# Five staging tiles instead of two for made weights, and their making spread over 49 or 50 steps of a block

## The chip, the cores and the metric

The kernel runs on one core of a Trainium2 chip. The metric is the device time of one execution in microseconds (us), median of several runs. A profile is one further execution, with its own time.

## The reference, cut to what matters

Attention with random features (4 batches, 8 heads, 576 positions, 64 per head) gives 2304 tokens of 512 numbers. Two layers follow, each with a hidden width of 2048:

```python
def reference(**kwargs):
    attn_out = _attn_ref(**attn_kwargs)
    x = np.ascontiguousarray(attn_out.transpose(0, 2, 1, 3)).reshape(B * S, H * D)
    x = _moe_ref(x=x, **moe_kwargs)       # h = x @ w_in; g = max(h,0) + alpha*min(h,0); g @ w_out
    return _moe2_ref(x=x, **moe2_kwargs)  # h = x @ w_in; r = max(h,0); (r*r) @ w_out
```

The weights w_in and w_out of both layers arrive as 64-bit numbers. The kernel turns them into 32-bit numbers by itself, and each number into a rounded part and a rest (hi and lo), so that three products on TensorE take the place of one exact product.

## The kernel before

**Blocks, turns, steps.** The 2304 tokens are three blocks of 768. A layer's hidden width is eight pairs of 256. The first layer runs three blocks (k = 0, 1, 2) of eight turns, one pair in each turn. In blocks 1 and 2 a turn has seven steps: seven products of 384 columns (a 2 by 2 scheme with seven instead of eight products, with operands such as A11, S1, T1), 42 matmuls in all, and between them the matmuls of the second product (`mm2`) of the pair before, 10 parts by the table `FILL`. So a block is 56 steps, numbered `turn * 7 + m`. Steps 1, 4 and 6 of a turn each have one VectorE (DVE) addition c = h + s, which reads a PSUM tile that a later product needs; ScalarE (ACT) copies s out of PSUM in steps 0, 2 and 4. Then come ReLU (ACT), slope r (DVE), high part gh (ACT) and rest gl (DVE), and `mm2` reads gh and gl.

**Order.** Every engine runs its instructions in the order in which the program writes them (`manual_schedule`). One DMA queue, SyncE's (SP), issues nearly all transfers, also in program order; raw weights are loaded by GpSimd's (POOL) queue into the part of x that is free in this block.

**Making weights.** Beside the matmuls the kernel makes the weights. `UNITS` lists the units of work; 9 to 16 are made in block 1, and 17 to 24 in block 2 (`ENDS`), all for the second layer. A unit loads two raw tiles of 512 KB (128 x 1024 x 4 bytes), scales and merges them to 32 bits (ACT, DVE, POOL), forms four sums, and so has eight matrices of 128 x 256. Seven of them are split into hi and lo (`cast` on ACT, `rest` on DVE) into a staging tile, and the staging tile is written to memory by SP (`keep`, `keep3`). A unit has ten positions (`SHORT`); `put(at, ...)` says what is done at which position. The staging tiles are `ma` (three matrices) and `ms` (four): `ma` is written at positions 5 to 8 and saved at 8; `ms` is written at 10 to 13 and saved at 13. The next unit's first cast into `ma` is at position 15, that into `ms` at 20; each must wait until the save has landed.

**Pace.** In blocks 1 and 2 the call of `upto` decides how many positions are done by each step:

```python
            elif layer == 0 and k and turn * 7 + m > (0, 5, 3)[k]:
                upto(end_of(ENDS[k - 1]) + (end_of(ENDS[k]) - end_of(ENDS[k - 1])) * (turn * 7 + m - (0, 5, 3)[k]) // (0, 44, 46)[k],
                     ENDS[k], k)
```

so the 80 positions of a block's eight units lie in steps 5 to 49 (block 1) and 3 to 49 (block 2).

**Reading.** In each turn whose next pair isn't held, SP reads that pair's made weights back: two halves of 896 KB and two of 512 KB. Turn 8 (`turn` 7) of block 1 reads nothing, since block 2 walks its pairs in the opposite direction.

**Operands of the next block.** The table `NEXT[1]` adds to steps 45 to 58 four differences (DVE), seven casts xh (ACT) and seven rests xl (DVE) of 768 columns, for the products of the block that follows. In the first turn of that block the result y is copied to x by ACT and DVE (line 904).

Of the kernel before, what the change touches and what calls it, by code (L numbers as in the profile page):

```python
# [10 lines left out]
F32R = mybir.dt.float32r  # L11
# [7 lines left out]
P = 128  # L19
# [16 lines left out]
QW = 2 * P  # L36
# [11 lines left out]
ENDS = (9, 17, 25)  # L48
# [6 lines left out]
def tile_performer_moe(ctx, tc, qt, kt, qn, kn, vn, omt, w1i, w1o, al, w2i, w2o, out):  # L55
# [38 lines left out]
    class Raw:  # L94
# [37 lines left out]
        def merge(self):  # L132
            nc.vector.scalar_tensor_tensor(
                out=self.high, in0=self.high, scalar=-0x80000000, in1=self.t, op0=ALU.bitwise_and, op1=ALU.bitwise_or)
            nc.gpsimd.tensor_tensor(out=self.out.bitcast(I32), in0=self.high, in1=self.low, op=ALU.add)  # L135

    def sums(names, outer=False):
        w = tiles["wf1"]
        a21, a22, a11, a12, s1, s2, s3, s4 = (w[:, n] for n in range(8))
        todo = {1: (s1, a21, a22, ALU.add), 2: (s2, s1, a11, ALU.subtract),  # L140
                3: (s3, a11, a21, ALU.subtract), 4: (s4, a12, s2, ALU.subtract)}
        if outer:

            b21, b22, b11, b12, t1, t2, t3, t4 = (w[:, n] for n in range(8))
            todo = {1: (t1, b12, b11, ALU.subtract), 2: (t2, b22, t1, ALU.subtract),
                    3: (t3, b22, b12, ALU.subtract), 4: (t4, b21, t2, ALU.subtract)}
        for n in names:
            o, a, b, op = todo[n]
            nc.vector.tensor_tensor(out=o, in0=a, in1=b, op=op)  # L149
# [6 lines left out]
    def made():  # L156
# [19 lines left out]
        def merge(raw):  # L176
            raw.merge()
            raws.remove(raw)
            fetch()
# [5 lines left out]
        def first(key, u, a0, a1):  # L185

            layer, p = key
            if layer == 0:
                return ring[p % 2][0][:, u, a0:a1]
            return tiles["ma"][:, u, a0 - A22:a1 - A22] if a1 <= S1 else tiles["ms"][:, u, a0 - S1:a1 - S1]  # L190

        def second(key, u, i):
            return ring[key[1] % 2][1][:, u, i]
# [7 lines left out]
        def keep(key, which, at, tile, queue=nc.sync):  # L201
            queue.dma_start(out=kept[key][which][:, :, at].bitcast(F32), in_=tile.bitcast(F32))

            if at in (0, slice(0, 7), slice(3, 7)):
                done.add((key, which))

        f1, f2 = tiles["wf1"], tiles["wf2"]

        def third(a0, a1):
            n, a = ("ma", 0) if a1 <= 3 else ("ms", 4)  # L210
            t = tiles[n].rearrange("p u n q -> p (u n q)").rearrange("p (n u q) -> p n u q", u=2, q=QW)
            return t[:, a0 - a:a1 - a]

        def cast3(a0, a1):
            high(third(a0, a1)[:, :, 0], f1[:, a0:a1])
# [5 lines left out]
        def keep3(p, a0, a1):  # L221
            n0 = a0 if a1 <= 3 else a0 - 1
            nc.sync.dma_start(out=outer[:, n0:n0 + a1 - a0, p].bitcast(F32), in_=third(a0, a1).bitcast(F32))
            done.add(((1, p), 1, n0))

        def cast1(key, a0, a1):
            high(first(key, 0, a0, a1), f1[:, a0:a1])

        def rest1(key, a0, a1):
            low(first(key, 1, a0, a1), f1[:, a0:a1], first(key, 0, a0, a1))  # L230
# [56 lines left out]
        def plan_unit(n, base):  # L287

            n1, n2 = UNITS[n]
            a, b = ((0, 0), (0, 1)) if n1 else ((1, 1), (1, 0))  # L290

            def put(at, *what):
                schedule[base + at] += what

            if n1:
                cast, rest, keeps = (lambda *r: cast1(n1, *r)), (lambda *r: rest1(n1, *r)), [
                    lambda: keep(n1, 0, slice(0, 3), tiles["ma"]), lambda: keep(n1, 0, slice(3, 7), tiles["ms"])]
                first_, second_ = (A11, S1), (A22, A11)
            else:
                cast, rest, keeps = cast3, rest3, [lambda: keep3(n2[1], 0, 3), lambda: keep3(n2[1], 4, 8)]  # L300
                first_, second_ = (0, 2), (2, 3)
            put(-1 if n not in ENDS else 0, lambda: used[n, *a].scale_high())
            put(0, lambda: used[n, *a].scale_low(), lambda: used[n, *a].shift())
            put(2, lambda: merge(used[n, *a]))
            put(3, lambda: used[n, *b].scale_high())
            put(4, lambda: used[n, *b].scale_low(), lambda: used[n, *b].shift())
            put(5, lambda: merge(used[n, *b]), lambda: cast(*first_))
            put(6, lambda: rest(*first_))
            put(7, lambda: cast(*second_), lambda: sums((1, 2), not n1))
            put(8, lambda: rest(*second_), keeps[0])  # L310
            put(9, lambda: sums((3, 4), not n1))
            put(10, lambda: cast(S1, S3))
            put(11, lambda: cast(S3, 8), lambda: rest(S1, S3))
            put(13, lambda: rest(S3, 8), keeps[1])

        for n in range(NPAIR + 1, len(UNITS)):
            plan_unit(n, (n - NPAIR - 1) * SHORT)
# [18 lines left out]
    def end_of(n):  # L336
        return min(n, NPAIR + 1) * STAGES + max(n - NPAIR - 1, 0) * SHORT + (4 if n == len(UNITS) else 0)
# [6 lines left out]
    def upto(where, most, blk):  # L344

        while position[0] < min(where, end_of(most)):
            onward(most, blk)
# [44 lines left out]
    def cast(k, n, of=operand):  # L392
        nc.scalar.copy(out=tiles["xh", n], in_=of(k, n))

    def rest(k, n, of=operand):
        nc.vector.tensor_tensor(out=tiles["xl", n], in0=of(k, n), in1=tiles["xh", n].bitcast(F32), op=ALU.subtract)  # L396
# [519 lines left out]
        for c in ("xh", "xl"):  # L916
            tiles[c, n] = xp.tile([P, 2, HB], F32R, name=f"{c}{n}")
    mr = making_room.enter_context(tc.tile_pool(name="mr", bufs=1, side="right", reuse_waits="tile"))
    for n, a in (("ma", 3), ("ms", 4)):
        tiles[n] = mr.tile([P, 2, a, QW], F32R, name=n)  # L920
    ring_end = ctx.enter_context(ExitStack())
    wp = ring_end.enter_context(tc.tile_pool(name="w2p", bufs=1, reuse_waits="tile"))
    ring[1].append(wp.tile([P, 2, 2, DM], F32R, name="w2_1"))
# [14 lines left out]
    for n, (layer, k, turn, p) in enumerate(plan):  # L938
        lead = plan[n + 1] if n + 1 < len(plan) else None
        held[p % 2] = layer, p  # L940
        reading = lead and lead[:2] != (0, 0) and held[lead[3] % 2] != (lead[0], lead[3])
        if layer:
            making_room.close()
            values(0)
        fill = enumerate(mm2(*before)) if before else iter(())
        full = []
        first = (layer, k) == (0, 0)
        steps = stepping.pop() if stepping else plain(p) if first else pair(layer, p)
        for m, got in enumerate(steps, DRAINED if n == 0 else 0):
            if reading and m in (0, 2):  # L950
                read(lead[0], lead[3], 0, m // 2)
            if layer and m == 0:
                for part in GROUPS:
                    read_pair(0, 1, part)
            if first and turn:

                upto((p + 1) * STAGES + STAGES * (m + 1) // 8 + 1, ENDS[0], 0)
            elif layer == 0 and k and turn * 7 + m > (0, 5, 3)[k]:
                upto(end_of(ENDS[k - 1]) + (end_of(ENDS[k]) - end_of(ENDS[k - 1])) * (turn * 7 + m - (0, 5, 3)[k]) // (0, 44, 46)[k],
                     ENDS[k], k)  # L960
            elif layer == 0 and k and m == (0, 5, 3)[k]:
                ask(ENDS[k], k)
            elif (layer, k, turn) == (0, 1, 0) and m < 2:

                onward(ENDS[0], 0)
            for blk, at in ((n // NPAIR, turn * (8 if first else 7) + m), (n // NPAIR - 1, NPAIR * 7 + turn * 7 + m)):

                table = NEXT[0 if blk == 0 else 1]
                at -= (NPAIR - 1) * (8 if blk == 0 and first else 7)
                if blk == 0 and not first:  # L970
                    at += 1
                if 0 <= blk < BLOCKS:
                    for what, operand_ in table.get(at, ()):
                        what((blk + 1) % BLOCKS, operand_)
            for rows in full:
                evacuate(ended, y, rows)
            full = []
            for _ in range(FILL[0 if first else 1][m]):
                part, _ = next(fill, (None, None))
                if turn == 0 and part is not None and part in COMPLETE:  # L980
                    full.append(COMPLETE[part])
        for part, _ in fill:
            if turn == 0 and part in COMPLETE:
                full.append(COMPLETE[part])
        for rows in full:
            evacuate(ended, y, rows)
        if turn == 0 and not layer:
            y = [py.tile([P, 512], F32, name=f"y{c}") for c in range(NB // P)]
        if reading and lead[0] == 0:
            read(lead[0], lead[3], 1, 1)  # L990
            read(lead[0], lead[3], 1, 0)
        before = turn, p, *got, y
        ended = k
# [281 lines left out]
```

## Time and profile before

| | |
|---|---|
| time, median of 3 runs | 905.99 us (902.18 to 906.78) |
| time of the profiled execution | 901.07 us, span 899.0 us |
| mean granted clock | 0.997 |
| TensorE (PE) busy | 881.9 us, 98% |
| VectorE (DVE), ScalarE (ACT), GpSimd (POOL) busy | 673.4, 522.6, 166.2 us |
| DMA | 228.81 MB, mean 255 GB/s |

PE's busy time counts a matmul from its start to a modelled end. What the kernel could win on PE is in its gaps, and a gap is read by what ended it, and by what that in turn waited for.

### The profile page before, as it was taken

Reading aid. Unit: us, or ns where it says so; the run is one execution under the profiler, and the core shown is the slowest. Engines: PE = TensorE matmul, PEld = TensorE weight load, DVE = VectorE, ACT = ScalarE, POOL = GpSimd, SP = SyncE. Lnnn points to the kernel's source line nnn. Section 1 sums busy time; section 2 is a strip of 40 time slices with the busy share of each in tenths; the row PEclk is TensorE's granted clock in tenths of the full one; section 3 lists DMA queues with packets and bytes.
Section 4 is the critical chain, followed back from the end, with each engine's and each line's share of the span. In section 5 each row is a group of like instructions: output and inputs, shape, how many; then the busy total and the mean of one; then the engine's idle time right before and its main releaser. Section 6 shows DMA issues by size and latency. Waiting matters only on the chain.

```text
span 899.0 us, 18473 instructions
## 1 busy us (share of the span) xinstructions
PE 881.9 (98%) x7328; PEld 834.8 (93%) x7328; DVE 673.4 (75%) x1077; ACT 522.6 (58%) x1109; POOL 166.2 (18%) x192
## 2 busy tenths in 40 slices
PE   9999999999999999999999999999999999999998
PEld 7998889999998888898898999999999999999998
DVE  5868987998986887877788974668855688657674
ACT  6889886777676666667676753334523245333432
POOL 6642322444412322202232100000000000000000
PEclk9999999999999999999999999999999999999999
DMA  7644316898836999927999975767697686876763
GB/s 272 196 139 144 120 30 219 293 303 284 291 141 227 348 399 375 337 92 291 393 348 366 369 266 168 249 249 264 235 309 250 205 322 251 268 259 228 297 249 135
DMA packets 82293, 228.81 MB, mean 255 GB/s; under 512 B 6176, under 2 KB 16800, under 8 KB 77216
## 3 DMA queue, kind: packets, MB, share of 16 engines
q1 hardware_dynamic: 72640, 192.21, 59.7%
q0 software_dynamic: 9216, 33.56, 11.2%
q10 hardware_dynamic: 352, 1.87, 0.6%
q8 instruction: 58, 0.95, 0.4%
q14 instruction: 27, 0.22, 0.1%
HBM read 170.47 MB, written 57.15 MB: 253 GB/s over the span
## 4 chain that ended last, share of the span: by engine, by line
PE 52%; DMA 2%; DVE 2%; ACT 1%; issue 0%; ACTq 0%; DVEq 0%
PE h L717 15%; PE sumb L717 10%; PE suma L1075 9%; PE sumc L1075 8%; PE y L886 7%; PE sumb L1075 3%; DMA k<-ms 2%; DVE r L754 0%; PE h L1075 0%; DVE wf L149 0%; DVE ma L199 0%; ACT x L123 0%; DVE gl L760 0%; DVE c L821 0%; DVE t L130 0%
## 5 line engine op out<-in xcount | busy, mean ns | idle before, releaser
L717 PE MATMUL h<-xh,w 128*128 128x384 f32 x1040 | 296.6, 338 | 6.2 <-ACT s L816 6.2
L717 PEld LDWEIGHTS h<-xh,w 128*128 128x128 f32 x1040 | 191.5, 188 | 10.5 <-ACT s L816 8.0
L886 PE MATMUL y<-gh,w 128*128 128x512 f32 (+1 forms) x768 | 176.9, 339 | 5.2 <-ACT gh L757 5.0
L717 PE MATMUL h<-xl,w 128*128 128x384 f32 x520 | 175.2, 337 | 0.2 <-DVE xl L396 0.2
L886 PEld LDWEIGHTS y<-gh,w 128*128 128x128 f32 x768 | 131.7, 189 | 18.2 <-ACT gh L757 6.8
L135 POOL TENSOR_TENSOR wf<-x 128x512 int32<-128x512 int32 x64 | 81.9, 1280 | 240.5 <-issue 43.5
L1089 ACT CAST gh<-g 128x768 fp32r<-128x768 f32 x72 | 56.6, 833 | 81.0 <-PE suma L1075 38.9
L886 PE MATMUL y<-gl,w 128*128 128x512 f32 (+1 forms) x384 | 103.6, 338 | 0.0
L717 PEld LDWEIGHTS h<-xl,w 128*128 128x128 f32 x520 | 98.0, 188 | 3.2 <-DVE xl L396 0.6
L717 PE MATMUL sumb<-xh,w 128*128 128x384 f32 x336 | 91.2, 335 | 0.0
L1091 DVE TENSOR_TENSOR gl<-g,gh 128x768 fp32r<-128x768 f32 x72 | 65.8, 955 | 32.2 <-PE suma L1075 17.2
L886 PEld LDWEIGHTS y<-gl,w 128*128 128x128 f32 x384 | 67.5, 188 | 9.2
L717 PEld LDWEIGHTS sumb<-xh,w 128*128 128x128 f32 x336 | 61.4, 188 | 0.2 <-ACT s L1021 0.2
L1075 PE MATMUL sumc<-w,gh 128*128 128x256 f32 x416 | 61.3, 283 | 0.0
L499 DVE TENSOR_REDUCE mx<-h 128x8 f32<-128x1024 f32 x36 | 44.0, 1223 | 21.9 <-PE h L486 21.4
L754 DVE SCALAR_TENSOR_TENSOR r<-n,al_sb,r 128x768 f32<-128x768 f32 x48 | 55.9, 1164 | 1.4 <-ACT r L749 1.4
L1075 PEld LDWEIGHTS sumc<-w,gh 128*128 128x128 f32 x416 | 56.5, 192 | 0.0
L717 PE MATMUL sumb<-xl,w 128*128 128x384 f32 x168 | 56.2, 335 | 0.0
L1075 PE MATMUL suma<-w,gh 128*128 128x256 f32 x432 | 54.8, 283 | 0.0
L760 DVE TENSOR_TENSOR gl<-r,gh 128x768 fp32r<-128x768 f32 x48 | 53.4, 1116 | 0.9 <-ACT gh L757 0.9
L1075 PEld LDWEIGHTS suma<-w,gh 128*128 128x128 f32 x432 | 53.1, 192 | 0.0
L821 DVE TENSOR_TENSOR c<-h,s 128x384 f32<-128x384 f32 x51 | 28.2, 553 | 30.6 <-PE h L717 17.8
(112 smaller groups left out, 1554.5 us busy)
## 6 DMA issues: line engine op xcount, KB each, us to landing
w<-k SPq DMA_DIRECT2D x99, 512.0 KB, 5.2
w<-k SPq DMA_DIRECT2D x39, 1024.0 KB, 4.9
w<-k SPq DMA_DIRECT2D x26, 896.0 KB, 9.0
k<-ms SPq DMA_DIRECT2D x16, 1024.0 KB, 7.8
k<-w SPq DMA_DIRECT2D x7, 1792.0 KB, 7.8
k<-ma SPq DMA_DIRECT2D x16, 768.0 KB, 7.0
x<-in_w1i POOLq DMA_DIRECT2D x16, 512.0 KB, 4.1
x<-in_w1o POOLq DMA_DIRECT2D x16, 512.0 KB, 5.3
```

Source lines behind the costliest of these rows:

```text
L135: nc.gpsimd.tensor_tensor(out=self.out.bitcast(I32), in0=self.high, in1=self.low, op=ALU.add)
L499: nc.vector.reduce_max(out=mx, in_=pj, axis=AX.X)
L717: nc.tensor.matmul(out, w[:, u, a, cs], tiles[v, b][:, kc], start=start and kc == 0 and j == 0, stop=stop and kc == 1 and j == 2, skip_gro ...
L754: nc.vector.scalar_tensor_tensor(out=r, in0=n, scalar=al_sb[:, f:f + 1], in1=r, op0=ALU.mult, op1=ALU.add)
L760: nc.vector.tensor_tensor(out=gl[:, i], in0=r, in1=gh[:, i].bitcast(F32), op=ALU.subtract)
L821: nc.vector.tensor_tensor(out=c, in0=b, in1=s, op=ALU.add)
L886: nc.tensor.matmul(y[a0 // 512][:, a0 % 512:a0 % 512 + a1 - a0], u[:, i, c * P:(c + 1) * P], v[:, i, ts], start=first and j == 0 and a0 % ...
L1075: nc.tensor.matmul(to[c], (l if v == 2 else h)[:, r, c * P:(c + 1) * P], w[:, rr, v % 2], start=fresh and rr == 0 and v == 0 and (c != 1 o ...
L1089: nc.scalar.copy(out=h[:, r], in_=f[:, r])
L1091: nc.vector.tensor_tensor(out=l[:, r], in0=f[:, r], in1=h[:, r].bitcast(F32), op=ALU.subtract)
```

## The change

The two staging tiles become a single (one matrix with hi and lo, 2 KB per partition) and four doubles (two matrices, 4 KB per partition): three new tiles in the same 14 KB, and as the fourth the tile `wf2`, which serves only the first layer's weights before. A unit takes three doubles in turn (`take`) and the single, and saves each as soon as its rest is done: four saves instead of two. Every cast and rest stands at the position where it stood before. The divisors of the pace become 50 (block 1) and 49 (block 2), so that the 80 positions lie in steps 5 to 55 and 3 to 52.

```diff
-            return tiles["ma"][:, u, a0 - A22:a1 - A22] if a1 <= S1 else tiles["ms"][:, u, a0 - S1:a1 - S1]
+            return staged(a0, a1)[:, u]
+
+        def staged(a0, a1):
+
+            return slots[a0].rearrange("p (u n q) -> p u n q", u=2, n=a1 - a0)
+
+        def take(a0, a1):
+
+            if a1 - a0 == 1:
+                slots[a0] = tiles["single"]
+            else:
+                slots[a0] = tiles["double"][taken[0] % 4]
+                taken[0] += 1
+
+        slots, taken = {}, [0]
...
+            def staging(a0, a1):
+
+                def begin():
+                    take(a0, a1)
+                    cast(a0, a1)
+
+                def end():
+                    rest(a0, a1)
+                    save(a0, a1)
+
+                return begin, end
+
+            (c1, r1), (c2, r2), (c3, r3), (c4, r4) = (staging(*at) for at in (first_, second_, (S1, S3), (S3, 8)))
...
-            put(5, lambda: merge(used[n, *b]), lambda: cast(*first_))
-            put(6, lambda: rest(*first_))
-            put(7, lambda: cast(*second_), lambda: sums((1, 2), not n1))
-            put(8, lambda: rest(*second_), keeps[0])
+            put(5, lambda: merge(used[n, *b]), c1)
+            put(6, r1)
+            put(7, c2, lambda: sums((1, 2), not n1))
+            put(8, r2)
             put(9, lambda: sums((3, 4), not n1))
-            put(10, lambda: cast(S1, S3))
-            put(11, lambda: cast(S3, 8), lambda: rest(S1, S3))
-            put(13, lambda: rest(S3, 8), keeps[1])
+            put(10, c3)
+            put(11, c4, r3)
+            put(13, r4)
...
-    for n, a in (("ma", 3), ("ms", 4)):
-        tiles[n] = mr.tile([P, 2, a, QW], F32R, name=n)
+    tiles["single"] = mr.tile([P, 2 * QW], F32R, name="ma")
+    tiles["double"] = [mr.tile([P, 4 * QW], F32R, name=f"ms{j}") for j in range(3)]
+    tiles["double"].append(tiles["wf2"].rearrange("p i n -> p (i n)").bitcast(F32R))
...
-                upto(end_of(ENDS[k - 1]) + (end_of(ENDS[k]) - end_of(ENDS[k - 1])) * (turn * 7 + m - (0, 5, 3)[k]) // (0, 44, 46)[k],
+                upto(end_of(ENDS[k - 1]) + (end_of(ENDS[k]) - end_of(ENDS[k - 1])) * (turn * 7 + m - (0, 5, 3)[k]) // (0, 50, 49)[k],
```

On SP's queue at the start of block 1, the saves of the first two units (targets k_1_0 and k_88) stand among the reads of the first layer's weights (targets w). Before:

```order
L368 DMA w_1_101<-k_0_5_69 128x1792 x2
L202 DMA k_1_0_72<-ma 256x1x768
L368 DMA w_1_2696<-k_5_85 128x2x512
L368 DMA w_0_100<-k_0_4_68 128x1792
L368 DMA w_1_2696<-k_5_85 128x2x512
L202 DMA k_1_0_72<-ms 256x1x1024
L368 DMA w_0_100<-k_0_4_68 128x1792
L223 DMA k_88<-ma 128x3x512
L368 DMA w_0_102<-k_4_84 128x2x512
L223 DMA k_88<-ms 128x4x512
```

With the change:

```order
L394 DMA w_1_101<-k_0_5_69 128x1792 x2
L216 DMA k_1_0_72<-ms_2692 256x1x512
L216 DMA k_1_0_72<-ma 256x1x256
L394 DMA w_1_2698<-k_5_85 128x2x512
L394 DMA w_0_100<-k_0_4_68 128x1792
L216 DMA k_1_0_72<-ms_2693 256x1x512
L394 DMA w_1_2698<-k_5_85 128x2x512
L216 DMA k_1_0_72<-ms_2694 256x1x512
L394 DMA w_0_100<-k_0_4_68 128x1792
L235 DMA k_88<-wf_99 128x2x512
L235 DMA k_88<-ma 128x512
```

Each save of a unit is now its own row, of half or a quarter of the size, and comes from a tile of its own until the ring of four doubles comes round.

On DVE, between the addition c of step 1 and that of step 4 in turn 8 of block 1 (t and x are the raw weights' shift and merge; wf, ms and ma the rests into staging; xl the rests of the next block's operands; gl the rest for `mm2`), there stands before:

```order
L760 TENSOR_TENSOR gl<-r,gh 128x768 x2
L396 TENSOR_TENSOR xl_1358<-x,xh_1357 128x768
L396 TENSOR_TENSOR xl_1360<-x,xh_1359 128x768
L821 TENSOR_TENSOR c<-h,s 128x384
```

With the change:

```order
L786 TENSOR_TENSOR gl<-r,gh 128x768
L130 TENSOR_SCALAR t<-x 128x512
L213 TENSOR_TENSOR wf_99<-wf_98,wf_99 128x512
L786 TENSOR_TENSOR gl<-r,gh 128x768
L133 SCALAR_TENSOR_TENSOR x<-x,t 128x512
L422 TENSOR_TENSOR xl_1358<-x,xh_1357 128x768
L213 TENSOR_TENSOR ms_2692<-wf_98,ms_2692 128x512
L130 TENSOR_SCALAR t<-x 128x512
L422 TENSOR_TENSOR xl_1360<-x,xh_1359 128x768
L847 TENSOR_TENSOR c<-h,s 128x384
```

Five instructions of the units now stand in this stretch, where before the units of the block had ended.

## Rows read from the trace of the kernel before

**Rows 1.** Waits over the whole span: engine, line, awaited; us in total, times, longest.

```profile
ACT ms L196 <- DMA k<-ms: 17.1, 7, 4.0
...
PE h L717 <- ACT s L816: 6.2, 5, 1.7
...
PE y L886 <- ACT gh L757: 5.0, 4, 2.0
```

**Rows 2.** PE's timeline, six gaps: start, us, instruction, idle before and what ended it.

```profile
306.13 0.44 PE L717 MATMUL h<-xh,w 128*128 128x384 f32 x1 [1.23 <-ACT s L816]
...
335.70 0.44 PE L717 MATMUL h<-xh,w 128*128 128x384 f32 x1 [1.36 <-ACT s L816]
...
348.87 0.98 PE L886 MATMUL y<-gh,w 128*128 128x512 f32 x4 [1.31 <-ACT gh L757]
...
374.87 0.45 PE L717 MATMUL h<-xh,w 128*128 128x384 f32 x1 [1.59 <-ACT s L816]
...
449.29 0.96 PE L886 MATMUL y<-gh,w 128*128 128x512 f32 x4 [2.01 <-ACT gh L757]
...
476.97 0.44 PE L717 MATMUL h<-xh,w 128*128 128x384 f32 x1 [1.72 <-ACT s L816]
```

**Rows 3.** ACT's timeline: first and one late of the seven waits for `ms`.

```profile
304.55 0.62 ACT L196 CAST ms<-wf 128x512 fp32r<-128x512 f32 x1 [4.03 <-DMA k<-ms]
...
475.38 0.62 ACT L196 CAST ms<-wf 128x512 fp32r<-128x512 f32 x1 [3.76 <-DMA k<-ms]
```

**Rows 4.** Windows: stretch; us, busy of PE, PEld, DVE, ACT, POOL; clock, DMA share, GB/s.

```profile
275.00:384.00 109.00, 102.52 (x577) 93.81 (x576) 87.84 (x144) 74.14 (x148) 27.72 (x29) 1.00 0.93 348
...
407.00:517.00 110.00, 105.42 (x590) 97.19 (x589) 90.72 (x151) 77.63 (x154) 28.12 (x29) 0.98 0.95 354
...
330.00:340.00 10.00, 8.64 (x48) 7.64 (x49) 8.28 (x14) 6.29 (x13) 4.00 (x4) 1.00 1.03 416
```

**Rows 5.** Page, part 6: transfers, KB of each, median us from issue to landing.

```profile
w<-k SPq DMA_DIRECT2D x99, 512.0 KB, 5.2
w<-k SPq DMA_DIRECT2D x39, 1024.0 KB, 4.9
w<-k SPq DMA_DIRECT2D x26, 896.0 KB, 9.0
k<-ms SPq DMA_DIRECT2D x16, 1024.0 KB, 7.8
...
k<-ma SPq DMA_DIRECT2D x16, 768.0 KB, 7.0
```

**Rows 6.** The chain that ended last, block 2: start us, us, what.

```profile
486.31 1.41 PE y L886 x8
...
498.31 2.10 PE h L717 x12
502.16 1.40 PE y L886 x8
```

**Rows 7.** Windows of 2 us after the gap at 449 us.

```profile
450.00:452.00 2.00, 2.00 (x10) 2.00 (x9) 2.00 (x4) 2.00 (x5) 0.19 (x1) 0.54 1.02 411
452.00:454.00 2.00, 2.00 (x9) 1.70 (x8) 2.00 (x3) 1.82 (x4) 1.70 (x2) 0.61 1.03 427
```

**Rows 8.** DVE's timeline in turn 7 of block 1: start, us, instruction.

```profile
366.45 0.55 DVE L821 TENSOR_TENSOR c<-h,s 128x384 f32<-128x384 f32 x1
366.92 0.94 DVE L760 TENSOR_TENSOR gl<-r,gh 128x768 fp32r<-128x768 f32 x1
367.79 0.87 DVE L149 TENSOR_TENSOR wf<-wf 128x256 f32<-128x256 f32 x2
368.57 0.42 DVE L199 TENSOR_TENSOR ma<-wf,ma 128x256 fp32r<-128x256 f32 x1
```

**Rows 9.** Line 368 (reads of the first layer's weights), all 50 transfers.

```profile
DMA to landing us min/median/max: 4.2/8.5/11.9
```

**Rows 10.** SP's timeline: a second half of a pair's reads.

```profile
488.27 0.52 SPq L368 DMA_DIRECT2D w<-k  x1
```

More of the change, by code (lines that the diff above doesn't have):

```diff
@@ L202, in keep @@
             queue.dma_start(out=kept[key][which][:, :, at].bitcast(F32), in_=tile.bitcast(F32))
-            if at in (0, slice(0, 7), slice(3, 7)):
+            if at in (0, slice(0, 7), slice(5, 7)):
                 done.add((key, which))
@@ L209, in third @@
         def third(a0, a1):
-            n, a = ("ma", 0) if a1 <= 3 else ("ms", 4)
-            t = tiles[n].rearrange("p u n q -> p (u n q)").rearrange("p (n u q) -> p n u q", u=2, q=QW)
-            return t[:, a0 - a:a1 - a]
+            return slots[a0].rearrange("p (n u q) -> p n u q", u=2, q=QW)
         def cast3(a0, a1):
@@ L295, in plan_unit @@
             if n1:
-                cast, rest, keeps = (lambda *r: cast1(n1, *r)), (lambda *r: rest1(n1, *r)), [
-                    lambda: keep(n1, 0, slice(0, 3), tiles["ma"]), lambda: keep(n1, 0, slice(3, 7), tiles["ms"])]
+                cast, rest = (lambda *r: cast1(n1, *r)), (lambda *r: rest1(n1, *r))
+                save = lambda a0, a1: keep(n1, 0, slice(a0 - A22, a1 - A22), staged(a0, a1))
                 first_, second_ = (A11, S1), (A22, A11)
             else:
-                cast, rest, keeps = cast3, rest3, [lambda: keep3(n2[1], 0, 3), lambda: keep3(n2[1], 4, 8)]
+                cast, rest, save = cast3, rest3, lambda *r: keep3(n2[1], *r)
                 first_, second_ = (0, 2), (2, 3)
+            def staging(a0, a1):
[7 more added lines that the diff above has]
+            (c1, r1), (c2, r2), (c3, r3), (c4, r4) = (staging(*at) for at in (first_, second_, (S1, S3), (S3, 8)))
             put(-1 if n not in ENDS else 0, lambda: used[n, *a].scale_high())
```

## The prediction

> **What bounds the kernel now.** First the table of busy times: PE is busy for 881.9 of 899.0 us, so nothing that saves work on another engine counts by itself, only what closes gaps of PE. The list of waits puts nearly all gaps down to two lines, 6.2 us to ACT's copy s and 5.0 us to ACT's cast gh [rows 1]. Both are only the last link. PE's timeline shows where: six gaps between 306 and 477 us, all in blocks 1 and 2 of the first layer, with 1.23 + 1.36 + 1.31 + 1.59 + 2.01 + 1.72 = 9.22 us [rows 2]. Ahead of each, ACT's own timeline has a cast into `ms` that waited until an earlier save of `ms` had landed, such as 4.03 us up to 304.55, with PE's gap ending at 306.13, and 3.76 us up to 475.38, with PE's gap ending at 476.97 [rows 2, 3]. There are seven such waits for `ms` with 17.1 us in all [rows 1]. The casts stand in ACT's program ahead of s and gh, so those come late. Two us of the 11.2 are left, where one block meets the next, with no save awaited.
>
> Why the saves land late is read from the windows. In the two stretches in which units are made, the DMA engines are 93% and 95% busy, with 348 and 354 GB/s; at 10 us with a gap in them the share is full and the rate 416 GB/s [rows 4]. So the rate at full share is 348 / 0.93 = 374 GB/s on the mean, and 416 at best. What a turn asks for: reads of 2 x 896 + 2 x 512 KB, and a unit 2 x 512 KB of raw weights and 768 + 1024 KB of saves [rows 5], each 2816 KB or 2.88 MB. A turn without gaps lasts 502.16 - 486.31 = 15.85 us [rows 6], a step 2.26 us. At 44 steps for eight units a turn has 7 / 5.5 = 1.27 units, so 6.55 MB in 15.85 us, 414 GB/s: all that the DMA engines gave at their best, and 11% over their mean. Blocks 1 and 2 are bound by DMA while units and reads run together, and the gaps are how that reaches PE.
>
> **The change, part by part.**
>
> *Pace.* At 50 steps a turn of block 1 has 1.12 units, 6.11 MB or 386 GB/s; in block 2 the step from 46 to 49 takes 403 to 390 GB/s. That lies between the mean of 374 and the best of 416, so it isn't free of queueing. In block 1, six turns with reads ask for 36.7 MB, which at 374 GB/s takes 98.1 us, 3.0 us more than the turns have; the turn behind them reads nothing and lets the queue run empty. In block 2 it is 6.18 MB in a turn, 16.5 us at 374 GB/s, 0.7 us behind in each of six or seven turns, 4 to 5 us at the end.
>
> *Staging.* What the queue can be behind before someone waits is set by the tiles. Before, `ma` is saved at position 8 and `ms` at 13, and written again at 15 and 20: seven positions of 15.85 x 5.5 / 70 = 1.25 us, so 8.7 us, against a median landing of 7.0 and 7.8 us [rows 5]. That is no reserve. Now the single has nine positions (8 to 17) and a double at least ten (11 to 21; the others 12 and 14), of 1.42 us in block 1 and 1.39 in block 2: 12.5 us and more. The transfers are smaller too. The reserve is some 5 us, as much as the queue falls behind in the worst block. So I take the 9.22 us as gone; the bounds are 0 and 9.22.
>
> *Clock.* Behind the gap of 2.01 us the granted clock fell to 0.54 and 0.61 in two windows of 2 us, so to the lower level of 1.2 GHz for most of that time, with PE busy throughout [rows 7]. That cost (0.46 + 0.39) x 2 = 1.7 us. Without the gap it goes; bounds 0 and 1.7.
>
> *Issuing.* SP gets 32 transfers more, at some 0.52 us of issue [rows 10], 17 us in 250 us, on a queue that mostly waits. The saves stand where they stood or earlier, and a read behind one waits for DVE's rest as before. I price this at nothing; SP's idle time covers it. Without that cover, a read would be up to 0.5 us later for each save. The reads have little reserve: a second half issued at 488.27 is used at 498.31, 10.0 us later, where the landing is 8.5 us on the median and 11.9 at worst [rows 6, 9, 10]. With the queue 3 to 5 us behind at the end of block 2, some reads may come late, which no row shows yet. Bounds: 0, and 3 us (once the whole lag, before the next turn's demand meets the delay). Since the saves now are what fills the queue, I take 1.0 us.
>
> *Late units.* Turn 8 of block 1 was free of units and has the next block's xl on DVE. Now ten positions, a whole unit, fall into it. Between the c of step 1 and that of step 4, DVE had 2 gl, 2 xl and c: with starts 0.87 us apart for a tile of 768 columns and 0.47 for c, 3.95 us [rows 8]. Now two shifts, a merge and two rests of 512 columns come to it; at twice a sum of 256 columns (0.78 us for two) the three large ones take about 0.65 each and the shifts 0.35, some 2.6 us more: 6.6 us, where PE needs about 5.2 (three products at 2.10 / 2 us and 2.1 us of `mm2`, of which 1.41 in step 2) [rows 6, 8]. Over the whole turn I count 16.4 us of DVE against PE's 15.85. PE waits only if c of step 4 isn't done at step 6, which is another 5 us later, so this lag of 1.4 us is mostly hidden. Late next are the additions c and slopes r of the turn's end, for gh. Bounds: 0, and 3.9 us if DVE idles there as it does in the stretch with units (87.84 of 109 busy [rows 4], and 16.4 / 0.81 = 20.3 us, 4.4 behind, less the reserve of 0.5 us at least). I take 0.5.
>
> *The sum.* 901.07 us is the profiled execution. 901.07 - 9.22 - 1.7 + 1.0 + 0.5 = 891.65. The three runs shown were 1.1 to 5.7 us above it, their median 4.9. If more or longer gaps and falls of the clock are behind that, it goes as well; if it is an offset, it stays. I add 2 of the 4.9: **893.6 us**. A median tells a change of 0.5%, 4.5 us, from none.
>
> **The rivals.**
>
> *DMA stays the bound* (A). The saves of the units of the outer kind keep their pieces, but those of the other kind fall from rows of 3 and 4 KB per partition to 2 and 1 KB. If the mean rate falls from 374 to 355 GB/s, block 1 and block 2 are behind by 5% more, 5 us each, and PE waits for reads or saves again. For it: 386 and 390 are over 374. Against it: 416 was reached, and block 1 has a turn to recover. Half of the 10.9 us would be left: 891.65 + 5.5 = 897, with the offset 899.
>
> *The units meet the next block's operands* (B). The upper bound of late units, 3.9 instead of 0.5, and a gap of over 2 us that lowers the clock as in [rows 7], 1.7: 891.65 + 5.1 = 896.8, with the offset 899. For it: DVE is over 100% asked for in that turn. Against it: the turn ahead of it is now lighter, so DVE enters it without a lag.
>
> *Nothing is gained* (C): the gaps move from saves to reads with the same length, since the same bytes go through the same engines; 901 to 906. Against it: block 1 now lets units run in a turn that has no reads.
>
> *Each transfer has its own price* (D), the case that ends slower. A read of 512 KB took 5.2 us to land and one of 1024 KB 4.9 [rows 5], so halving a transfer didn't halve its time. If the price held the DMA engines, 16 more transfers in a block would cost. A block can lose what it has in reserve (5 us) and what it gains (5.5 us), so the point is 10.5 / 16 = 0.66 us for each; above it the kernel is slower. At 2 us a block loses 32 - 10.5 = 21.5 us, and the time is 906 + 43 = 949. Against it: at full share 416 GB/s went through in a mixture of sizes, and four landings that were one behind the other in a unit, 3 x 5.2 us and a smaller one, would be more than its 14 us, where the landings before, 7.0 + 7.8 = 14.8 us, already were more than a unit's 12.4; so landings overlap, and their length is no occupancy. The Trainium skill has a rule that would speak for this case (DMA: Bandwidth & Descriptors, section on the anatomy of one DMA): about 2.0 us fixed for each transfer, and half of the bandwidth only from some 860 KB. By that rule as occupancy, the estimate would be 32 x 2.0 = 64 us of DMA time more; that page of the Trainium skill itself puts most of the 2 us down to waiting for the receipt of the write, and by that it is latency, which the longer reserve of the tiles covers. The overlap of landings in the trace agrees with the second reading.
>
> **How the numbers follow.** The forecast has 0.70, A 0.10, B 0.07, C 0.08, D 0.05. The likeliest alone lies between 888 (all 11.2 us of gaps and the clock's 1.7 go, no offset) and 898 (all of the offset, 4.9, and the small costs at 2.5). For the range I go from 888 to 901, which takes in A and B and leaves out C, D and the tail. Faster by over 0.5% means under 901.5: the forecast, A, B, and little of C, 0.69 + 0.06 + 0.05 = 0.80 after a deduction for the offset; within 0.5% 0.13; slower 0.07.
>
> **What would show it.** Right: no wait of ACT for `ms` or `ma` of over 1 us, no gap of PE between 290 and 480 us, DMA share below full in more windows of block 1 and some share in its turn 8, the granted clock at full in block 2, the first layer's end some 10 us earlier, and the second layer unchanged. Wrong: PE waits for a transfer w<-k (A, C), gaps at the last turn of block 1 behind DVE's xl or c (B), or landings of the small saves of 10 us and more with the DMA share full (D).

## The result, and the profile after

The changed kernel takes 894.62 us (median of 4 runs, 891.05 to 898.08) against 906.32 us; the ratio is 0.9874, 95% interval 0.983 to 0.9918. Forecast were 893.6 us and a gain. The sum behind it was right in its sign and its main term, but two terms were mis-sized and one step was wrong, as the experiments show.

The profiled execution took 896.34 us, span 894.6. Its page, parts 1 and 6:

```profile
PE 882.8 (99%) x7328; PEld 837.2 (94%) x7328; DVE 672.6 (75%) x1077; ACT 523.1 (58%) x1109; POOL 167.1 (19%) x192
...
k<-ms SPq DMA_DIRECT2D x36, 512.0 KB, 7.3
```

The landing of a save has hardly become shorter: 7.3 us for 512 KB against 7.8 for 1024 [rows 5]. Yet in blocks 1 and 2 no cast waits for a save any more, and the six gaps [rows 2] are gone. PE's timeline has these gaps left (start, us, instruction, idle before and its releaser):

```profile
18.93 1.64 PE L512 MATMUL h<-om,raw 64*128 64x128 f32 x16 [2.96 <-ACT e L537]
...
275.12 0.44 PE L743 MATMUL h<-xl,w 128*128 128x384 f32 x1 [0.26 <-DVE xl L422]
...
287.59 0.97 PE L912 MATMUL y<-gh,w 128*128 128x512 f32 x4 [0.85 <-ACT gh L783]
...
387.41 0.44 PE L743 MATMUL h<-xh,w 128*128 128x384 f32 x1 [0.81 <-ACT s L842]
...
399.75 0.96 PE L912 MATMUL y<-gh,w 128*128 128x512 f32 x4 [0.54 <-ACT gh L783]
404.46 0.44 PE L743 MATMUL h<-xh,w 128*128 128x384 f32 x1 [0.23 <-ACT s L842]
...
417.15 0.96 PE L912 MATMUL y<-gh,w 128*128 128x512 f32 x4 [0.84 <-ACT gh L783]
```

The three from 387 to 405 us lie in and behind turn 8 of block 1, where the units now meet the next block's operands. The gap at 18.93 us is in the attention, which the change doesn't touch.

Windows of 10 us (busy of PE, PEld, DVE, ACT, POOL; clock, DMA share, GB/s) answer to [rows 4]:

```profile
330.00:340.00 10.00, 10.00 (x59) 9.46 (x58) 8.80 (x15) 7.72 (x15) 2.72 (x4) 1.00 1.04 401
...
390.00:400.00 10.00, 9.46 (x54) 8.54 (x53) 9.91 (x17) 6.26 (x13) 1.64 (x1) 1.00 0.35 129
...
450.00:460.00 10.00, 10.00 (x59) 9.27 (x59) 8.25 (x13) 6.81 (x15) 3.48 (x4) 1.00 1.04 410
```

The DMA share is as full as before, but between 290 and 380 us and between 420 and 510 us PE is busy throughout. In turn 8 of block 1 (390 to 400) it isn't, and DVE is full there.

**A measure without the start's scatter.** DVE's first copy of y into x (line 904, in the change 930) marks the same point in each block: 277.97, 412.96 and 544.66 us before, 285.06, 414.61 and 540.64 after. Their differences are block 1 and block 2; the start is read at PE's gap behind xl (268.04 us before). The first of these copies, before and after:

```profile
277.97 1.94 DVE L904 COPY x<-y 128x256 f32<-128x256 f32 x4
285.06 1.94 DVE L930 COPY x<-y 128x256 f32<-128x256 f32 x4
```

Worked out so from each profile, in us, beside the times:

```
kernel   time, median  ratio (95% interval)      start  block 1 block 2  sum
before   903.8 - 906.3 1                         268.0  134.99  131.70  266.69
after    894.62        0.9874 (0.983 - 0.9918)   275.1  129.55  126.03  255.58
both     895.65        0.9877 (0.984 - 0.9915)   274.3  129.58  126.04  255.62
staging  891.33        0.984  (0.9802 - 0.9877)  273.8  127.21  125.84  253.05
pace     897.13        0.9912 (0.9874 - 0.9949)  276.6  132.37  127.40  259.77
noread   899.14        0.9942 (0.9907 - 0.9977)  272.5  131.09  130.01  261.10
saves4   897.94        0.991  (0.9878 - 0.9941)  280.5  129.32  127.56  256.88
ring3    892.83        0.9865 (0.9824 - 0.9906)  271.4  129.13  125.78  254.91
halves   892.82        0.9877 (0.9814 - 0.9939)  270.0  128.76  126.84  255.60
extra    906.24        1.0003 (0.9973 - 1.0033)  268.9  135.13  131.78  266.91
p4449    892.03        0.9861 (0.9799 - 0.9923)  270.9  127.16  126.03  253.19
p4746    890.28        0.9858 (0.9784 - 0.9932)  267.8  128.59  126.03  254.62
nonext   893.01        0.9863 (0.9803 - 0.9923)  274.5  127.13  126.11  253.24
later    888.04        0.9808 (0.9777 - 0.9839)  269.2  128.11  125.95  254.06
```

What comes behind block 2 takes 353.9 to 354.7 us in every kernel. Two profiles of the same program (after, both) agree within 0.04 us in the blocks, while the start scatters by 13 us. At the old pace the agreement is less close: `later` differs from `staging` only ahead of block 1 and takes 1.01 us more in the two blocks. PE waits there for reads, which it doesn't in `staging`:

```profile
PE h L743 <- DMA w<-k: 0.4, 2, 0.2
```

So at the old pace, a difference of 1 us in the blocks is within what two profiles show.

### The profile page after: what moved, and what is told of

Its sections match the earlier page's. It is cut to its first block, busy times and chain, and to the rows that moved or that the text cites. A ratio compares the mean times of both kernels' runs of the same rounds, so it can differ in the third digit from the quotient of the medians.

```text
span 894.6 us, 18587 instructions
## 1 busy us (share of the span) xinstructions
PE 882.8 (99%) x7328; PEld 837.2 (94%) x7328; DVE 672.6 (75%) x1077; ACT 523.1 (58%) x1109; POOL 167.1 (19%) x192
## 3 DMA queue, kind: packets, MB, share of 16 engines
q0 software_dynamic: 9216, 33.56, 11.4%
## 4 chain that ended last, share of the span: by engine, by line
PE 90%; DVE 5%; ACT 3%; issue 1%; DMA 1%; DVEq 0%; ACTq 0%
PE h L743 27%; PE y L912 19%; PE sumb L743 10%; PE suma L1102 9%; PE sumc L1102 8%; PE h L512 4%; PE sumb L1102 3%; PE t L632 2%; PE o L664 2%; PE t L519 2%; PE o L558 2%; PE t L651 1%; DVE r L780 1%; DMA x<-in_w1i 1%; ACT e L537 1%
## 5 line engine op out<-in xcount | busy, mean ns | idle before, releaser
L783 ACT CAST gh<-r 128x768 fp32r<-128x768 f32 x48 | 40.1, 835 | 16.8 <-DVE r L780 16.6
```

The source lines that it names most:

```text
L783: nc.scalar.copy(out=gh[:, i], in_=r)
```

## The experiments

**The two halves of the change, and the load on the DMA engines.** `both` is the changed kernel again; `staging` has the five tiles and the old pace; `pace` the two old tiles and the new pace; `noread` is the kernel before without the reads of w2.

```diff
 staging (from after):  -// (0, 50, 49)[k]   +// (0, 44, 46)[k]
 pace (from before):    -// (0, 44, 46)[k]   +// (0, 50, 49)[k]
 noread (from before):
-        if reading and lead[0] == 0:
-            read(lead[0], lead[3], 1, 1)
-            read(lead[0], lead[3], 1, 0)
```

> The changed kernel once more, beside the other three on one chip. If its gain is real it comes out at 891 to 898 us, with no wait of the casts for a save, and the kernel before at 902 to 907.

> The five staging tiles with the old pace of 44 and 46 steps. Theory (transfers are over-asked, and the tiles' reserve decides from when somebody waits): a turn asks for 414 GB/s, the queue falls some 10 us behind in block 1, the reserve is 11 us less a landing of 7 to 8; part of the waits stays, 4 to 12 us of them, and the time is 897 to 902. Rival, only the reuse of the tiles matters: no waits, 891 to 897. Rival, only the pace matters: 902 to 907.

> The old two staging tiles with the pace of 50 and 49 steps. Theory: 386 and 390 GB/s asked for, seven positions of 1.4 us are 9.9 us against landings of 7 to 8; most waits go but some stay, 3 to 8 us, and the time is 895 to 900. Rival, only the tiles matter: 902 to 907. Rival, only the pace matters: 891 to 897.

> The kernel before, without the reads of the first layer's second weights in blocks 1 and 2 (12 times 2 x 512 KB left out, so stale weights are used there). Theory: a turn asks for 5.5 MB less a little, 350 GB/s at most, which is under the mean rate of 374; the saves land in time even with two tiles and the old pace, the waits for ms and ma fall from 22 us to under 4, PE's six gaps go, and the time is 891 to 897. Rival, the landing of a save against the reuse of its tile is what counts whatever else is moved: the waits stay at 15 us and more, 902 to 907.

`staging` is faster than the whole change: 13.6 us less than before in the two blocks, against 11.1 with the pace. That is the rival's number, not mine. Its windows in block 2:

```profile
440.00:450.00 10.00, 10.00 (x59) 9.33 (x58) 9.05 (x14) 8.11 (x16) 1.90 (x2) 1.00 1.04 412
490.00:500.00 10.00, 10.00 (x58) 9.33 (x57) 9.88 (x18) 7.88 (x16) 2.20 (x2) 1.00 1.05 413
```

I had worked out that the old pace asks for 403 GB/s in block 2 (414 in block 1); 412 go through with PE at 10.00. The mean of the whole stretch is over 374 GB/s as well:

```profile
412.00:520.00 108.00, 107.16 (x611) 99.36 (x610) 92.61 (x149) 78.30 (x155) 27.03 (x27) 1.00 1.01 385
```

So 374 GB/s was no limit of the DMA engines. `pace` alone takes 6.9 us off the blocks, and its time is in the range given. Its waits are not: 3 to 8 us were expected, and there are 16.9.

```profile
ACT ms L196 <- DMA k<-ms: 10.9, 6, 4.7
...
ACT ma L196 <- DMA k<-ma: 6.0, 3, 4.0
```

`noread`, with 12.6 MB fewer to move, was to have under 4 us of waits:

```profile
ACT ms L196 <- DMA k<-ms: 13.0, 6, 4.6
...
ACT ma L196 <- DMA k<-ma: 6.7, 5, 3.0
```

It has 19.7 us, near the 22 of before (17.1 for `ms` [rows 1], 4.9 for `ma`), and gains only 5.6 of the 13.6 us in the blocks. Its time, 899.1 us, lies between the two ranges that I had given. The load is lower on the mean of the stretch with units, 0.78 and 290 GB/s where before had 0.93 and 348 [rows 4]:

```profile
282.00:391.00 109.00, 105.26 (x596) 96.98 (x595) 92.39 (x150) 77.68 (x155) 27.93 (x29) 1.00 0.78 290
```

Lower load helps, but the old tiles wait at a lower mean load too. (It isn't lower everywhere: in the 10 us of the first wait, 300 to 310, the share is still 1.00.) My theory fell; the next was that the time between a save and the next write of its tile against the landing is what counts.

**What of the staging.** `saves4` keeps the two old tiles and saves the change's four pieces at the change's positions; `ring3` takes only three doubles.

```diff
 saves4 (from before, and alike at 8, 11 and 13):
-            put(6, lambda: rest(*first_))
+            put(6, lambda: rest(*first_), lambda: save(*first_))
 ring3 (from staging):
-                slots[a0] = tiles["double"][taken[0] % 4]
+                slots[a0] = tiles["double"][taken[0] % 3]
```

> The two old tiles and the old pace, but each tile saved in the change's pieces, each as soon as its rest is done: four saves a unit at the same positions as in the change. Revised theory (what counts is the time from a save to the next write of its tile against the landing, not the load on the DMA engines): a piece has 8 or 9 positions, 10 to 11 us, against 8.7 before; if a cast waits only for the piece that it overwrites, the waits fall under 6 us and the block times come near those of the five tiles; if it waits for all saves of its tile, the last piece still has only 7 positions, and the waits stay at 12 us and more, 899 to 905. Rival, the number of transfers or their size matters and not the reserve: block times as with the five tiles in any case.

> Five staging tiles less the fourth double (wf2 isn't taken), old pace. Reserve of a double 9, 9 and 8 positions of 1.25 us, of the single 9: 10 to 11 us. Revised theory: that is over nearly all landings (median 7 to 8, longest 11.5), so waits of 0 to 4 us and a time 0 to 3 us above the one with four doubles, 890 to 895. Rival, the fourth double is what the gain hangs on: most waits come back, 898 to 905.

`saves4` gets 9.8 of the 13.6 us with no new tile. Its waits:

```profile
ACT ms L196 <- DMA k<-ms: 3.8, 2, 1.9
ACT ma L196 <- DMA k<-ma: 3.4, 2, 1.8
...
DVE ms L199 <- DMA k<-ms: 1.4, 2, 0.8
DVE ma L199 <- DMA k<-ma: 1.1, 1, 1.1
```

These 9.7 us lie between my two cases. The trace shows why: a write waits for the pieces that it overwrites and not for the whole tile, but units of two kinds take turns, which lay hi and lo out differently in the tile. ACT, two casts into `ms`, and the rest that follows the second:

```profile
342.06 0.62 ACT L196 CAST ms<-wf 128x512 fp32r<-128x512 f32 x1 [1.92 <-DMA k<-ms]
354.87 0.60 ACT L196 CAST ms<-wf 128x512 fp32r<-128x512 f32 x1
356.02 0.69 DVE L199 TENSOR_TENSOR ms<-wf,ms 128x512 fp32r<-128x512 f32 x1 [0.76 <-DMA k<-ms]
```

The cast at 354.87 starts while a save of the same tile is still on its way; only the rest at 356.02 waits for that one. In such a unit (saved at line 202) the hi part of a piece overwrites one old piece and the lo part another; in the other kind (line 223) the hi parts overwrite two, so the cast waits for the last save. All four waits of casts are of that kind. So half of the units kept the old reserve in `saves4`, and it doesn't separate the reserve from the smaller pieces. `ring3` does: it has the pieces of `staging` and less reserve. It has three waits of 3.4 us in all, longest 1.6, and one gap of PE more than `staging` (1.48 us): the sum is 1.9 us higher. With 8 or 9 positions of reserve for the doubles (10 to 11 us) waits are rare; with 10 and more, and 9 for the small single, there are none in `staging` (in `later` one of 0.3 us, for the single). That fits the theory.

**The price of a transfer, and the DMA engines' limit.** `halves` splits nearly every save of `staging` in two, 56 transfers more with the same bytes; `extra` saves one double of each unit a second time.

```diff
 halves: +                    for u in range(2):
         +                        nc.sync.dma_start(out=kept[n1][0][:, u, at].bitcast(F32), in_=staged(a0, a1)[:, u].bitcast(F32))
 extra:  +                    if a0 == S3:
         +                        nc.sync.dma_start(out=spill.pop().bitcast(F32), in_=slots[a0].bitcast(F32))
```

> Five staging tiles and old pace, each save split in two transfers (the singles of the outer units stay whole): 60 transfers more, same bytes, same rows. The case of a price for each transfer: at 0.66 us or more of DMA time for each, blocks 1 and 2 are over 30 us more together. Theory: no such price, 889 to 894, block times within 1 us.

> Five staging tiles and old pace, with the last double of each unit saved a second time to memory that nobody reads: 0.5 MB more for each unit, 7.2 MB or 456 GB/s asked for in a turn with reads. Over-asked theory at the best rate seen (about 416): 1.5 us behind in each turn, 9 us in a block, over the reserve, so waits for saves or reads and gaps of PE return late in the blocks, 895 to 903. If the DMA engines are far from being the bound even so: 889 to 894, and no waits.

`halves` is 2.55 us above `staging` in the blocks and 1.54 above `later`, whose saves are whole. That is 0.03 to 0.05 us for each transfer, hardly told from the 1.01 us between those two: no price of the size of case D. It shows, as in `later`, in PE waiting for a read:

```profile
PE h L750 <- DMA w<-k: 1.7, 3, 0.8
```

`extra` gives back all of the gain, by the same wait and a lower granted clock behind two of its gaps (0.83 in the window from 360 us, 0.88 and 0.95 from 460):

```profile
PE h L746 <- DMA w<-k: 9.5, 5, 3.7
```

Its full windows move 409 to 411 GB/s, no more than `staging` does:

```profile
440.00:450.00 10.00, 10.00 (x59) 9.30 (x58) 7.67 (x14) 6.77 (x14) 1.25 (x2) 1.00 1.03 411
480.00:490.00 10.00, 10.00 (x58) 9.34 (x57) 8.66 (x14) 7.37 (x16) 2.23 (x2) 1.00 1.05 409
```

So some 412 GB/s is what the engines give for this mixture, `staging` runs at it, and past it (456 asked for) the reads come late first. `later` shows that the old pace with whole saves already touches it.

**Where the pace costs.** `p4449` has the new pace in block 2 alone, `p4746` half of the overlap in turn 8; `nonext` is the changed kernel without the 18 operand instructions of block 2.

```diff
 p4449:  -// (0, 50, 49)[k]   +// (0, 44, 49)[k]
 p4746:  -// (0, 50, 49)[k]   +// (0, 47, 46)[k]
 nonext: -                if 0 <= blk < BLOCKS:
         +                if 0 <= blk < BLOCKS and blk != 1:
```

> Five staging tiles, block 1 at its old pace (44 steps), block 2 at the new one (49). Theory (the pace costs only in turn 8 of block 1, where the units meet the next block's operands): block 1 as with the old pace, 127.2 us between the copies of y, block 2 as with the new, 126.0; time 889 to 893. Rival, the new pace costs by itself, wherever it is: the sum of both blocks stays over 255.

> Five staging tiles, block 1 with 47 steps (about five positions, half of a unit, fall into turn 8 instead of ten), block 2 at its old pace. Theory: one of the three gaps at most, block 1 between 127.3 and 128.8 us; time 889 to 894. If the cost doesn't depend on what meets in turn 8: 129.5.

> The changed kernel without the differences, casts and rests that make block 2's operands in and behind turn 8 of block 1 (18 instructions on ACT and DVE left out, so block 2 computes with block 1's operands). Theory: the units alone don't fill turn 8, the gaps behind s and gh there go, block 1 takes 127.3 us or less, time 888 to 893. Rival, the units' own spreading (or the transfers in turn 8) makes the gaps: block 1 stays at 129 and more.

All three came as the theory had it (the time of `nonext` is 0.01 us above its range): block 1 takes 127.16 us with its old pace, 128.59 with half of the overlap, 129.55 with all of it, and 127.13 with all of it but without the operands. In `p4746` one gap is left in turn 8:

```profile
380.05 0.45 PE L743 MATMUL h<-xh,w 128*128 128x384 f32 x1 [0.59 <-ACT s L842]
```

Both causes are needed, the units and the operands.

**The start.** In most profiles ACT comes to the first raw weights before they have landed. In the changed kernel's ACT timeline:

```profile
16.14 0.66 ACT L123 ACTIVATE x<-x 128x512 f32<-128x512 f32 x1 [2.99 <-DMA x<-in_w1i]
```

The gap of 2.96 us that ends at 18.93 us above follows. Right behind it the granted clock goes to the lower level for some 10 us: in windows of 2 us it is 0.86 from 18, 0.50 from 20 to 28, 0.58 from 28 and 1.00 again from 30 us. (My expectation below has the fall from 28 us on; in this profile it is over by 30.) Before and after, 20 to 60 us:

```profile
20.00:60.00 40.00, 39.63 (x966) 36.65 (x962) 30.17 (x56) 32.82 (x119) 24.40 (x29) 1.00 0.50 157
20.00:60.00 40.00, 39.63 (x858) 36.59 (x858) 29.16 (x54) 30.67 (x108) 22.82 (x28) 0.88 0.48 146
```

`later` is `staging` with the first unit's work one attention step later.

```diff
-MAKE_K = 2
+MAKE_K = 3
```

> Five staging tiles, old pace, and the first unit's work begins one attention step later (MAKE_K 3 instead of 2), so that ACT doesn't come to the first raw weights at 13 us, before they have landed. Theory: the gap of PE near 18 us behind ACT's e, found in most profiles of all versions, and the lower clock from 28 us on come from that wait; both go, the stretch to the operands of block 1 is 267 to 269 us as in the kernel's before best execution, the time is 886 to 889 and scatters less. Rival, the fall of the clock in the first 40 us has nothing to do with it: the stretch stays at 270 to 276 in most executions, 889 to 893.

It has the lowest median, 888.04 us (886.33 to 890.93, 6 runs), 0.9808 of before, though its interval overlaps that of `staging`. Its profile has the clock at 1.00 throughout; at the end of the fall, where `both` has 0.71, `later` has:

```profile
28.00:30.00 2.00, 2.00 (x58) 1.86 (x56) 1.21 (x5) 1.44 (x6) 1.27 (x2) 1.00 0.78 249
```

and of `both`:

```profile
28.00:30.00 2.00, 2.00 (x38) 1.76 (x38) 0.75 (x1) 0.45 (x2) 0.08 (x1) 0.71 0.37 131
```

ACT still waits 1.64 us for that transfer, at 17.60 us, so the cause isn't wholly taken away, and the start is 269.2 us, just above the range given. That the wait brings the lower clock rests on more than this pair. In nine of the fourteen profiles PE has a gap of 1.77 to 4.29 us behind such a wait, and in all nine the granted clock falls to 0.50 in the gap or within 2 us behind it, for 3 to 24 us. In the other five, with no gap or one of 0.90 to 1.95 us, it stays at 1.00. Five of the six runs of `later` have a mean clock of 1.000 over the whole span, against one of five of `staging`; its scatter (4.6 us) is no smaller than that of `staging` (3.8).

## Why the prediction was right, and where it was not

**What bounds the kernel.** The chain from the save over the cast to s or gh and to PE was right: with the waits gone, the six gaps are gone. The step "Blocks 1 and 2 are bound by DMA while units and reads run together" was wrong. 374 GB/s, taken for the rate at full share, was no bound: `staging` moves 385 GB/s over block 2 without a wait. Nor had the waits lowered it, since GB/s divided by share gives 381 for `staging` as well; the rate at full share differs with what is moved. `noread` shows that the two tiles wait at a lower mean load too. What I had named in passing, "no reserve" of 8.7 us against landings of 7 to 8, was what decided. The DMA engines are near their limit, as `extra` shows, but with room enough they make no such waits.

**Staging.** I took the 9.22 us of gaps and 1.7 us of clock as gone, 10.9 us. `staging` alone gave 13.6. The idle that went is 9.22 and another 0.31 us, with the clock 11.2; the other 2.4 us are about 0.34 for each of seven gaps. PE's idle is counted from modelled ends of matmuls that overlap (starts 0.17 us apart, 0.34 us long), so a gap loses the overlap as well; that this is the 0.34 us is argued from the rows, not shown by a run, and the single gap of `p4746`, 0.59 us, goes with 1.38 us in block 1, so it is no constant.

**Pace.** I priced it as part of the gain. Alone it is worth 6.9 us; beside the tiles it is worth nothing and costs 2.5.

**Late units.** Priced at 0.5 us of 0 to 3.9; it measured 2.34 in block 1 (129.55 - 127.21), from the three gaps of 1.58 us and their overlap. That DVE would be full was right, though not each price: twice a sum of 256 columns is 0.78 us and not the 0.65 that I took, and a rest of 512 columns measured 0.69 us, or up to 1.53. For the first gap I took c on DVE for the last link, "mostly hidden". It was ACT. Its timeline in the changed kernel, turn 8, steps 0 to 2:

```profile
383.71 0.53 ACT L774 ACTIVATE n<-c 128x384 f32<-128x384 f32 x1 [0.47 <-DVE c L847]
384.14 0.51 ACT L775 ACTIVATE r<-c 128x384 f32<-128x384 f32 x1
384.56 0.60 ACT L210 CAST wf<-wf 128x512 fp32r<-128x512 f32 x1
385.07 0.68 ACT L126 ACTIVATE x<-x 128x512 int32<-128x512 uint32 x1
385.64 0.61 ACT L210 CAST ms<-wf 128x512 fp32r<-128x512 f32 x1
386.15 0.83 ACT L419 CAST xh<-x 128x768 fp32r<-128x768 f32 x1
386.89 0.47 ACT L842 COPY s<-h 128x384 f32<-128x384 f32 x1
```

Three instructions of the units and one xh stand between r and s without a break, and s ends at 387.36, where PE's gap ends. The gap at 399.75 is the one that I had named as next, gh behind c and r: ACT waits 2.67 us for that c.

**Late reads.** I took 1.0 us; it is 0, as PE waits for no read in the changed kernel. `later`, `halves` and `extra`, all at the old pace, show that this wait is indeed the next. Issuing, priced at nothing, cost nothing that a row shows.

**Offset.** I added 2 of the 4.9 us between the profiled execution of before and the median. The start explains such a difference: 268.0 us in that execution, 267.8 to 280.5 in the others, with parts of the program that no change touches before `later`. It stays, so all of it should have been added. By the measured terms the sum is 901.07 - 11.1 + 4.9, about 895.

So the number held partly by luck: the larger gain of the tiles and the larger costs of the pace and the offset nearly cancel. Of the signs that I had named, two failed. The DMA share in block 1 stayed full instead of falling below it, and block 1 has gaps of PE (387 to 405 us). The first layer ends 4 us earlier in the profile, 11 less the later start, where I had said 10.

**The rivals.** A was to be half of the gain lost to waits: there were none. B happened, with 2.3 us instead of 3.9 and without a fall of the clock there. C fell. D fell to 0.05 us for each transfer at most. The rule of the Trainium skill (DMA: Bandwidth & Descriptors, the anatomy of one DMA) of about 2 us fixed, which the page gives for transfers issued by GpSimd while these saves go by SP's queue, agrees with the runs only as latency: 256 KB saves in `halves` still land in 7.6 us, and 56 more transfers cost 2.55 us in all.

## What to carry to other kernels

A mean rate in a stretch with waits isn't the limit of the engines that are waited for: take away the load and, apart from it, the lack of room, and see which of them ends the waits. A staging buffer is sized by its time from save to next write against the longest landing (here 11.2 us and more against up to 11.4 in `staging`), and then work needn't be slowed down. Read a fall of the clock in windows short enough to see where it begins. Before work is spread into a quieter stretch, list on every engine, in order, what stands ahead of the copies that PE waits for.

## What the runs showed of the hardware

One core's DMA engines moved 409 to 413 GB/s of reads and writes in pieces of 256 KB to 1 MB for 67 us (three of the 22 us slices of `staging`), and no more when 456 were asked for (`extra`). The rate at full share is not one number: windows of 10 us with a share of 1.03 have 365 GB/s (changed kernel, from 310 us) and 405 to 410 (`staging`). Splitting saves into 56 more transfers cost 1.5 to 2.6 us in all. A gap of PE of 1.8 to 4.3 us behind a wait for one early transfer goes with a granted clock of 0.50, the lower of its two levels, from some 18 or 20 us on, for up to 24 us (`saves4`); that moves the whole time by more than half of the change's gain.

In the changed kernel's timeline the same rest on DVE takes 0.69 us or more than twice as long. It is long where it starts while POOL's add of a merge (line 135) runs: it then ends 0.55 us behind that add. That holds for 31 of the 32 such rests of blocks 1 and 2 in the traces of before, after and `staging`; all others take 0.68 or 0.69 us.

```profile
385.19 0.69 DVE L213 TENSOR_TENSOR wf<-wf,wf 128x512 fp32r<-128x512 f32 x1 [0.31 <-ACT wf L210]
...
387.59 1.53 POOL L135 TENSOR_TENSOR wf<-x 128x512 int32<-128x512 int32 x1 [11.74 <-DVE x L133]
388.14 1.53 DVE L213 TENSOR_TENSOR ms<-wf,ms 128x512 fp32r<-128x512 f32 x1
```
